# Parameter columns by a transposing DMA, stores of two chunks on ScalarE, and the skip product of chunk 0 on VectorE

## The chip, the cores and the metric

The kernel runs on one core of a Trainium2 chip. The metric is the device time of one execution in microseconds (us). Every ratio below compares a kernel with the kernel before on the same chip in the same rounds. The experiments ran in four such groups (e1 to e4, e5 to e8, e9 to e12, e13 and e14), each on another chip, so kernels of different groups are compared by their ratios. A run that takes over 1.5% more than the fastest of its own kernel is called slow and is left out of the ratio. A difference under 2% is called faster or slower only where the 95% interval of the ratio leaves out 1.

The words for the engines: TensorE is PE in the profile (PEld is its weight load), VectorE is DVE, ScalarE is ACT, GpSimd is POOL, SyncE is SP. A trailing q (ACTq, SPq, POOLq) is that engine's sequencer, which issues DMAs and waits for semaphores.

## The reference

```python
def reference(x, Lambda, B, C, log_dt, Dskip, w_gate, w_up, w_down):   # cut
    xn = layernorm(x)                        # 2048 tokens x 448
    dt = exp(log_dt); Lam_bar = exp(dt * Lambda)
    Bu = xn @ (((Lam_bar - 1) / Lambda)[:, None] * B).T
    h_t = Lam_bar * h_{t-1} + Bu_t           # complex scan over 2048 tokens
    s = 2 * real(h @ C.T) + xn * Dskip       # the last term is "the skip"
    g = silu((silu(xn @ w_gate) * (xn @ w_up)) @ w_down)   # F = 1792
    return x + s * g
```

## The kernel before

The 2048 tokens go through in four chunks of 512, each of four tiles of 128 tokens. Per chunk TensorE does the projections `pb` (input of the scan), the feed-forward pair `gp` and `up` ("gu"), the down product `hd` and the output sum `y`. Weights and states of 448 rows are split into 64-row halves of the array:

```python
def tell(mm):                       # a "notice": an empty instruction of GpSimd
    told = nc.gpsimd.nop(nofuse=True)
    tc.add_manual_dep(told.ins, mm.ins.name, SYNC, reason="share")
    return told.ins.name

def sums(q, pairs, between=None):   # cut: the two halves of the array take turns
    for share, first in ((0, True), (1, False)):
        for n, two in enumerate(pairs):
            for m in range(4 - share):
                for half in range(2):
                    mm = nc.tensor.matmul(...)
                    if not first and m == 0:
                        told_of(mm, left[n])      # second share waits for the notice
            if first:
                left.append(tell(mm))             # first share done: GpSimd passes it on
        if first:
            run_power()                           # one queued power, also on GpSimd
```

Every bank's second share waits until GpSimd has passed on a notice. GpSimd also computes the roots of the layer norm:

```python
def act_root(q):                    # sums come from ScalarE
    nc.gpsimd.tensor_scalar(out=vep[...], in0=sums_of[:, 1, :], ...)
    nc.gpsimd.tensor_tensor(out=rstd[...], in0=vep[...], in1=halves[:], op=ALU.pow)
    nc.gpsimd.tensor_tensor(out=off_of[:, 1, :], in0=off_of[:, 0, :], in1=rstd[...], op=ALU.mult)
```

The parameters (four rows of 448) are loaded as rows by GpSimd and turned into columns by six small transposes on TensorE, in the middle of `second_tokens`. The output tiles:

```python
def finish(q, j, y, sg, eng=nc.sync, c0=0, c1=D):       # cut
    t = work.tile(...)
    if (q, j) in SKIPS:                                  # chunks 1 to 3, not the last tile
        nc.vector.tensor_tensor(out=t[:], in0=y, in1=skip[q][:, j, c0:c1], op=ALU.add)
        y = t[:]
    nc.vector.tensor_tensor(out=t[:], in0=y, in1=sg[:, c0:c1], op=ALU.mult)
    ob = work.tile([P, c1 - c0], BF16, name="ob", **of)  # two buffers
    nc.vector.tensor_tensor(out=ob[:], in0=t[:], in1=x_all[:, m, c0:c1], op=ALU.add)
    eng.dma_start(out=out2d[m * P : (m + 1) * P, c0:c1], in_=ob[:])
```

For the tiles not in SKIPS, TensorE adds the skip itself with four matmuls against a diagonal, per tile. The middle of the schedule, in program order (cut):

```python
sg = downs(0, 1.8, {0: ..., 1: ..., 2: act_sums((10, 11), 1) + [on(act_root, 2), on(skips, 1)]})
bg.finish(0); turned_norms(8, 9, 10, 11)
outs(0, sg)                                             # stores by SyncE
sg = downs(1, 2.4, {0: act_sums((12, 13, 14), 0) + [on(skips, 2)],
                    1: act_sums((15,), 0) + [act_means] + act_sums((12, 13), 1),
                    2: act_sums((14, 15), 1) + [on(act_root, 3)]})
drive(2, 4.8)                                           # the projections pb of chunk 2
gu(2, bg, 2.4)
```

Of the kernel before, what the change touches and what calls it, by code (L numbers as in the profile page):

```python
# [10 lines left out]
ALU = mybir.AluOpType  # L11
ACT = mybir.ActivationFunctionType
BF16 = mybir.dt.bfloat16
F32 = mybir.dt.float32
# [30 lines left out]
def kernel(  # L45
# [43 lines left out]
    def blk(k):  # L89
        return slice(k * P, k * P + P) if k < KF else slice(D - P, D)  # L90
# [16 lines left out]
    def ctile(shape, dtype, name):  # L107
        return const.tile(shape, dtype, name=name)
# [13 lines left out]
    Id = ctile([P, P], BF16, "Id")  # L122
    CT = ctile([P, KT, W], BF16, "CT")
    ST = ctile([P, KT, W], BF16, "ST")
    vrow = ctile([4, D], BF16, "vrow")
    xn = [ctile([P, KT * P], BF16, f"xn{i}") for i in range(TQ)]
    pcol = ctile([P, KT + 1, 4], F32, "pcol")
    it_f = work.tile([P, W], F32, name="it_f", tag="row", bufs=1)
# [40 lines left out]
    natC = [work.tile([P, KT, D], BF16, name="natC", tag="nz") for _ in range(2)]  # L169
    nc.vector.memset(Wd[:, 0, :], 0.0)  # L170
    nc.vector.memset(Id[:], 0.0)
    nc.vector.memset(half_pi[:], math.pi / 2)
    for h, v in ((slice(0, R), TWO_PI), (slice(R, P), -TWO_PI)):
        nc.vector.memset(two_pi[h], v)

    def warm(n):
        t = bank("warm")
        for _ in range(n):
            nc.tensor.matmul(t[:, 0:D], lhsT=Wd[:, 0, 0:P], rhs=Wd[:, 0, :], start=True, stop=True)
# [76 lines left out]

    sums_of = ctile([P, 2, TQ], F32, "sums_of")
    off_of = ctile([P, 2, TQ], F32, "off_of")

    def act_sum(n, squares):  # L260
        i = n % TQ
# [33 lines left out]
    def ln_transpose(n):  # L295
        tp = bank("tp", BF16)
        for k in range(KT):
            nc.tensor.transpose(tp[:, block(k)], xn[n][:, blk(k)], Id[:])
        return tp

    def ln_evacuate(n, tp, eng):
        tp = tp[:, 0 : KT * P].rearrange("p (k c) -> p k c", k=KT)
        if eng is nc.scalar:
            nc.scalar.activation(xT_of(n), tp, ACT.Copy)  # L304
        else:
            nc.vector.tensor_copy(out=xT_of(n), in_=tp)
# [9 lines left out]
    dtv = vnew("dtv")  # L316
    b_re, b_im, nb_im = vnew("b_re"), vnew("b_im"), vnew("nb_im")

    def transpose_state(out, src, k, ident):

        if k < KF:
            nc.tensor.transpose(out, src[:, blk(k)], ident)
        else:
            for h in (slice(0, R), slice(R, P)):
                nc.tensor.transpose(out[h], src[:, KF * P : D], ident)

    def params_row(t):

        tv = t[:, KT * P : KT * P + 4 * (KT + 1)].rearrange("p (k r) -> p k r", r=4)
        for k in range(KT + 1):  # L330
            if k < KT:
                transpose_state(tv[:, k, :], vrow, k, Id[0:4, 0:4])
            else:
                nc.tensor.transpose(tv[:, k, :], vrow[:, blk(KF)], Id[0:4, 0:4])
        return tv

    def params_in():
        tt, ts = nc.vector.tensor_tensor, nc.vector.tensor_scalar
# [264 lines left out]
        return sg  # L603

    skip = {}
    SKIPS = [(q, j) for q in (1, 2, 3) for j in range(TQ)][:-1]

    def skips(q):

        skip[q] = work.tile([P, TQ, D], BF16, name="skip", tag="nz")  # L610
        for j in range(TQ):
            for c0, c1, x0 in ((0, KF * P, 0), (KF * P, D, KF * P + R)):
                nc.vector.tensor_tensor(
                    out=skip[q][:, j, c0:c1], in0=xn[j][:, x0 : x0 + c1 - c0],
                    in1=skip["row"][:, c0:c1], op=ALU.mult,
                )

    def out_sum(q, j, k0=0, k1=KT):

# [34 lines left out]
    def on(fn, *args):  # L654
        return lambda: fn(*args)
# [5 lines left out]
    for n in range(2):  # L661
        ln_norm(n)
        ln_evacuate(n, ln_transpose(n), nc.scalar)
        warm(1 + n)
    for n in range(2, TQ):
        ln_stats(n)
        ln_root(n, n + 1)
# [2 lines left out]

    def second_tokens():
        ln_evacuate(2, ln_transpose(2), nc.scalar)
        t = ln_transpose(3)
        tv = params_row(t)
        ln_evacuate(3, t, nc.vector)
        nc.scalar.activation(pcol[:], tv, ACT.Copy)
        power(dtv[:], euler[:], pcol[:, 0:KT, 0])

    CW = W // 2
# [37 lines left out]
    def drive(q, budget):  # L717
        bu_alloc(q)
        bu(q, (0, 1, 2), True, [on(table_sin, 3), params_trig] if q == 0 else ())
        if q == 0:  # L720
            params_out()
        ssm_steps(bg, q)
        bg.run(budget)

# [6 lines left out]
            bg.run(budget)  # L731
        return sg

    def outs(q, sg, hooks={}):
        for j in range(len(sg)):
            finish(q, j, out_sum(q, j), sg[j])
            for fn in hooks.get(j, ()):
                fn()

    def do(fns):  # L740
        for fn in fns:
            fn()

    gu(0, bg, 0.0, {
        0: [*stats(4, 5), on(params_in), on(table_phase, 0)],
# [15 lines left out]
    def act_sums(ns, squares):  # L761
        return [on(act_sum, n, squares) for n in ns]

    gu(1, bg, 2.2, {2: cw(0)[0], 3: cw(0)[1], 4: cw(1)[0], 5: cw(1)[1]})
    drive(1, 4.0)
    sg = downs(0, 1.8, {
        0: cw(2)[0] + cw(3)[0] + act_sums((8, 9), 0),
        1: act_sums((10, 11), 0) + [act_means] + act_sums((8, 9), 1) + cw(2)[1] + cw(3)[1],
        2: act_sums((10, 11), 1) + [on(act_root, 2), on(skips, 1)],
    })  # L770
    bg.finish(0)
    turned_norms(8, 9, 10, 11)
    outs(0, sg)
    sg = downs(1, 2.4, {
        0: act_sums((12, 13, 14), 0) + [on(skips, 2)],
        1: act_sums((15,), 0) + [act_means] + act_sums((12, 13), 1),
        2: act_sums((14, 15), 1) + [on(act_root, 3)],
    })
# [1 line left out]
    gu(2, bg, 2.4)  # L780
    bg.finish(1)
    turned_norms(12, 13, 14, 15)
    outs(1, sg)
    sg = downs(2, 2.4, {1: [on(skips, 3)]})
    drive(3, 4.8)
    gu(3, bg, 2.4)
    bg.finish(2)
# [36 lines left out]
```

## Time and profile before

| | before |
|---|---|
| median of 4 runs | 187.42 us (186.88 to 187.54) |
| span of the profiled run | 185.0 us, TensorE clock 1.000 |
| TensorE busy | 177.9 us, 96% |
| first pb / pb of chunk 2 / last y start at | 29.82 / 89.04 / 179.46 us |

The span is cut into 40 slices by the profile page, and each engine's busy share is given per slice; the timeline of one engine lists its instructions with start, duration and, in brackets, the idle time just before with the instruction that ended it. Two places of the kernel before are shown here because the result turns on them. The first is the table of stretches for the start (columns: stretch; busy time and count of PE, PEld, DVE, ACT, POOL; granted TensorE clock; DMA share; GB/s).

```profile
10.50:15.30 4.80, 4.71 (x68) 3.05 (x66) 2.88 (x7) 2.50 (x6) 1.02 (x1) 1.00 1.03 323
15.30:21.20 5.90, 5.88 (x58) 2.46 (x54) 5.62 (x18) 4.75 (x10) 1.19 (x1) 1.00 0.92 253
```

TensorE is busy in all of it at full clock, while the DMA engines are saturated with the weight loads. The second place is GpSimd's timeline around the third root.

```profile
88.92 1.01 POOL L278 TENSOR_TENSOR rstd<-vep,halves 128x4 f32<-128x4 f32 x1
90.00 0.22 POOL L281 TENSOR_TENSOR off_of<-off_of,rstd 128x4 f32<-128x4 f32 x1
```

```profile
89.04 5.47 PE L455 MATMUL pb<-xT,BT 64*128 64x512 bf16 x56
```

The projections of chunk 2 start at 89.04 us. Their first shares (16 of 56 matmuls) take at most 1.90 us, as the row of the changed kernel below shows, so TensorE needs the first notice shortly before 90.94. GpSimd dispatches the last instruction of the root at 90.00. The slack of that notice is therefore only some 0.8 us, an estimate from these starts.

### The profile page before, as it was taken

The page shows a single profiled execution, that of the slowest core. Times are in us where ns is not written, and L with a number is a line of the kernel's source. Part 1 is how long each engine was busy: PE and PEld are TensorE (multiplying, and loading weights), DVE is VectorE, ACT ScalarE, POOL GpSimd, SP SyncE. Part 2 cuts the span into 40 slices and gives each one's busy share as a digit, 9 for nine tenths or more (in the row PEclk, how much of TensorE's full clock was granted, in tenths as well). Part 3 has the DMA queues.
Part 4 walks back from the last instruction along what each step waited for, and adds up shares of the span by engine and source line. Part 5 has one row for each costly group of instructions (what it writes and reads, how often), then busy time and mean ns, then how long its engine had stood idle before and what let it go on. Part 6 is the DMA issues. An engine that isn't in the chain of part 4 may idle for free.

```text
span 185.0 us, 3723 instructions
## 1 busy us (share of the span) xinstructions
PE 177.9 (96%) x1449; PEld 87.8 (47%) x1449; DVE 160.1 (87%) x254; ACT 120.2 (65%) x247; POOL 13.4 (7%) x25
## 2 busy tenths in 40 slices
PE   7899999999999999999999999979999999999991
PEld 3574444544444555555454444535454444455551
DVE  4649799999999999902999999999999999999583
ACT  3247879997789999498499556962259696512110
POOL 7332200000000000600300000000000000000000
PEclk9999999999999999999999999999999999999999
DMA  5899655979200000043100000042100000001111
GB/s 160 209 277 338 124 94 112 132 167 377 101 0 0 5 0 0 0 86 81 50 2 4 2 0 4 0 82 70 62 4 0 0 4 0 0 4 50 50 50 50
DMA packets 26129, 12.71 MB, mean 69 GB/s; under 512 B 16000, under 2 KB 26112, under 8 KB 26112
## 3 DMA queue, kind: packets, MB, share of 16 engines
q1 hardware_dynamic: 24896, 12.06, 25.3%
q10 hardware_dynamic: 1088, 0.41, 0.8%
q8 instruction: 11, 0.18, 0.4%
q14 instruction: 6, 0.05, 0.1%
q0 software_dynamic: 128, 0.00, 0.0%
HBM read 7.23 MB, written 1.84 MB: 49 GB/s over the span
## 4 chain that ended last, share of the span: by engine, by line
PE 67%; DVE 25%; DMA 3%; issue 2%; ACT 1%; POOL 0%; SPq 0%; DVEq 0%
PE gp L455 20%; PE hd L597 16%; PE up L455 15%; PE pb L455 9%; PE y L626 7%; DVE bu_re L527 5%; DVE bu_im L527 4%; DVE tmp L521 2%; DVE Vt L589 2%; DVE ob L648 2%; DMA out_dram<-ob 2%; DVE t L645 2%; DVE H_im L521 2%; DVE ere L521 1%; DMA x_all<-in_A_x_dram 1%
## 5 line engine op out<-in xcount | busy, mean ns | idle before, releaser
L455 PE MATMUL gp<-xT,Wg 64*128 64x512 bf16 (+1 forms) x413 | 85.8, 365 | 0.4 <-ACT xT L304 0.3
L455 PE MATMUL up<-xT,Wu 64*128 64x512 bf16 (+1 forms) x413 | 85.8, 365 | 0.0
L455 PEld LDWEIGHTS <-Wg 64*128 64x128 bf16 x413 | 38.5, 94 | 25.1 <-issue 0.4
L455 PEld LDWEIGHTS <-Wu 64*128 64x128 bf16 x413 | 38.4, 94 | 19.7 <-POOLq L437 0.5
L581 ACT ACTIVATE gs<-gp 128x512 bf16<-128x512 f32 x56 | 33.7, 604 | 19.6 <-PE gp L455 11.7
L597 PE MATMUL hd<-Wd,Vt 128*128 128x448 bf16 x224 | 43.4, 353 | 1.3 <-DVE Vt L589 1.3
L585 ACT ACTIVATE us<-up 128x512 bf16<-128x512 f32 x54 | 32.9, 609 | 0.0
L597 PEld LDWEIGHTS <-Vt 128*128 128x128 bf16 x224 | 21.8, 98 | 22.0 <-DVE Vt L589 1.7
L602 ACT ACTIVATE sg<-hd 128x448 bf16<-128x448 f32 x16 | 8.6, 538 | 25.2 <-PE hd L597 20.6
L455 PE MATMUL pb<-xT,BT 64*128 64x512 bf16 (+1 forms) x224 | 21.9, 349 | 0.0
L648 DVE TENSOR_TENSOR ob<-t,x_all 128x448 bf16<-128x448 f32 (+2 forms) x17 | 10.2, 597 | 8.2 <-DMA out_dram<-ob 7.7
L589 DVE TENSOR_TENSOR Vt<-gs,us 128x2048 bf16<-128x2048 bf16 (+1 forms) x16 | 17.2, 1079 | 0.0
L455 PEld LDWEIGHTS <-BT 64*128 64x128 bf16 x224 | 10.7, 94 | 11.4 <-issue 0.7
L626 PE MATMUL y<-C,H_re 128*128 128x448 bf16 (+2 forms) x68 | 15.7, 342 | 0.0
L527 DVE TENSOR_TENSOR_SCAN bu_re<-rcol,H_re,ere 128x512 bf16<-128x512 f32 x12 | 14.9, 1262 | 0.1
L488 ACT ACTIVATE bu_re<-pb 128x512 bf16<-128x512 f32 (+1 forms) x20 | 10.1, 537 | 2.7 <-PE pb L455 2.6
L626 PE MATMUL y<-C,H_im 128*128 128x448 bf16 (+2 forms) x51 | 11.9, 342 | 0.0
L498 ACT ACTIVATE bu_im<-bu_re 64x512 bf16<-64x512 bf16 x16 | 10.0, 628 | 2.1 <-DVE bu_re L527 1.8
L527 DVE TENSOR_TENSOR_SCAN bu_im<-rcol,H_im,eim 128x512 bf16<-128x512 f32 x9 | 11.4, 1262 | 0.0
L287 ACT ACTIVATE xn<-x_all,off_of,rstd 128x384 bf16<-128x384 bf16 (+1 forms) x16 | 8.1, 588 | 2.8 <-POOL off_of L281 2.8
L521 DVE TENSOR_TENSOR tmp<-bu_im,ST 128x2048 bf16<-128x2048 bf16 x8 | 9.7, 1218 | 0.0
L626 PEld LDWEIGHTS <-H_re 128*128 128x128 bf16 x68 | 6.4, 98 | 6.1 <-issue 0.4
(98 smaller groups left out, 174.5 us busy)
## 6 DMA issues: line engine op xcount, KB each, us to landing
out_dram<-ob SPq DMA_DIRECT2D x15, 112.0 KB, 1.7
Wd<-in_B_w_down_dram SPq DMA_DIRECT2D x1, 1568.0 KB, 9.0
x_all<-in_A_x_dram SPq DMA_DIRECT2D x1, 896.0 KB, 5.5
Wg<-in_B_w_gate_dram SPq DMA_DIRECT2D x2, 384.0 KB, 7.0
Wu<-in_B_w_up_dram SPq DMA_DIRECT2D x2, 384.0 KB, 7.6
x_all<-in_A_x_dram SPq DMA_DIRECT2D x1, 448.0 KB, 5.7
Wg<-in_B_w_gate_dram SPq DMA_DIRECT2D x1, 288.0 KB, 3.1
Wu<-in_B_w_up_dram SPq DMA_DIRECT2D x1, 288.0 KB, 4.2
```

The source lines that it names most:

```text
L455: mm = nc.tensor.matmul(out, lhsT=w[h, d, :], rhs=xT[h, d, q * W + c0 : q * W + c1], start=(first and m == 0), stop=(not first and m == 3 ...
L488: nc.scalar.activation(to, pair[i][0], ACT.Copy)
L498: nc.scalar.activation(out[a], in_[b], ACT.Copy)
L521: nc.vector.tensor_tensor(out=of(out, n), in0=of(a, n), in1=of(b, n), op=op)
L527: nc.vector.tensor_tensor_scan(out=T["b"][c][:, k, :], data0=rcol[:, k : k + 1].to_broadcast([P, W]), data1=T["e"][c][:, k, :], initial=in ...
L581: nc.scalar.activation(gs[:, i + j, :], gp_[:], ACT.Silu)
L585: nc.scalar.activation(us[:, i + j, :], up_[:], ACT.Copy)
L589: nc.vector.tensor_tensor(out=Vt[:, f0 : f0 + n, :], in0=gs[:, 0:n, :], in1=us[:, 0:n, :], op=ALU.mult)
L597: nc.tensor.matmul(hd, lhsT=Vt_of[q][:, fi, j * P : (j + 1) * P], rhs=Wd[:, fi, :], start=(fi == 0), stop=(fi == NF - 1),)
L602: nc.scalar.activation(sg[:], hd, ACT.Silu)
L626: nc.tensor.matmul(y[:, c0:c1], lhsT=h, rhs=C2[:, n, c0:c1], start=(n == 0), stop=(n == NS - 1))
L648: nc.vector.tensor_tensor(out=ob[:], in0=t[:], in1=x_all[:, m, c0:c1], op=ALU.add)
```

## The change

The intent: take six small transposes and sixteen diagonal matmuls from TensorE, which is 96% busy, and take the stores of chunks 0 and 1 out of SyncE's queue, where they stand behind transposing DMAs and make VectorE wait 7.7 us for an output buffer.

```diff
-    vrow = ctile([4, D], BF16, "vrow")
+    vrow = work.tile([16, D], BF16, name="vrow", tag="ob")
+    vcol = ctile([P, KT, 16], BF16, "vcol")
...
+    nc.vector.memset(vrow[:], 0.0)
...
-    def transpose_state(...) / params_row(t): six nc.tensor.transpose      # cut
+    def turn_params():
+        for k, cols in ((slice(0, KF), slice(0, KF * P)), (slice(KF, KT), blk(KF))):
+            nc.scalar.dma_start(out=vcol[:, k, :], in_=vrow[:, cols], transpose=True)
+
+    def params_col():                      # four small ScalarE copies, cut
...
         ln_evacuate(n, ln_transpose(n), nc.scalar)
         warm(1 + n)
+    turn_params()
...
     def second_tokens():
         ln_evacuate(2, ln_transpose(2), nc.scalar)
-        t = ln_transpose(3)
-        tv = params_row(t)
-        ln_evacuate(3, t, nc.vector)
-        nc.scalar.activation(pcol[:], tv, ACT.Copy)
+        ln_evacuate(3, ln_transpose(3), nc.vector)
+        params_col()
         power(dtv[:], euler[:], pcol[:, 0:KT, 0])
...
-    SKIPS = [(q, j) for q in (1, 2, 3) for j in range(TQ)][:-1]
+    SKIPS = [(q, j) for q in range(NQ) for j in range(TQ)][:-1]
+    def first_norms():                     # four ScalarE normalisations of chunk 0, cut
...
-    sg = downs(0, 1.8, {
+    sg = downs(0, 1.3, {
...
-        2: act_sums((10, 11), 1) + [on(act_root, 2), on(skips, 1)],
+        2: act_sums((10, 11), 1) + [on(act_root, 2), on(skip_tile, 0), on(skip_tile, 1),
+                                    first_norms, on(skips, 1)],
+        3: [on(skips, 0)],
...
-    outs(0, sg)
+    outs(0, sg, nc.scalar)
...
-    outs(1, sg)
+    outs(1, sg, nc.scalar)
```

More of the change, by code (lines that the diff above doesn't have):

```diff
@@ L258 @@
     off_of = ctile([P, 2, TQ], F32, "off_of")
+    off_0 = ctile([P, TQ], F32, "off_0")
     def act_sum(n, squares):
@@ L317 @@
     b_re, b_im, nb_im = vnew("b_re"), vnew("b_im"), vnew("nb_im")
-    def transpose_state(out, src, k, ident):
-        if k < KF:
-            nc.tensor.transpose(out, src[:, blk(k)], ident)
-        else:
-            for h in (slice(0, R), slice(R, P)):
-                nc.tensor.transpose(out[h], src[:, KF * P : D], ident)
-    def params_row(t):
-        tv = t[:, KT * P : KT * P + 4 * (KT + 1)].rearrange("p (k r) -> p k r", r=4)
-        for k in range(KT + 1):
-            if k < KT:
-                transpose_state(tv[:, k, :], vrow, k, Id[0:4, 0:4])
-            else:
-                nc.tensor.transpose(tv[:, k, :], vrow[:, blk(KF)], Id[0:4, 0:4])
-        return tv
+    def turn_params():
+        for k, cols in ((slice(0, KF), slice(0, KF * P)), (slice(KF, KT), blk(KF))):
+            nc.scalar.dma_start(out=vcol[:, k, :], in_=vrow[:, cols], transpose=True)
+    def params_col():
+        last = vcol[:, KF, 0:4]
+        nc.scalar.activation(pcol[:, 0:KF, :], vcol[:, 0:KF, 0:4], ACT.Copy)
+        nc.scalar.activation(pcol[:, KT, :], last, ACT.Copy)
+        for h in (slice(0, R), slice(R, P)):
+            nc.scalar.activation(pcol[h, KF, :], last[R:P], ACT.Copy)
     def params_in():
@@ L605, with skip_tile @@
     skip = {}
-    SKIPS = [(q, j) for q in (1, 2, 3) for j in range(TQ)][:-1]
+    SKIPS = [(q, j) for q in range(NQ) for j in range(TQ)][:-1]
+    def skip_tile(q):
+        skip[q] = work.tile([P, TQ, D], BF16, name="skip", tag="nz")
     def skips(q):
-        skip[q] = work.tile([P, TQ, D], BF16, name="skip", tag="nz")
         for j in range(TQ):
-            for c0, c1, x0 in ((0, KF * P, 0), (KF * P, D, KF * P + R)):
+            parts = [(0, KF * P, 0), (KF * P, D, KF * P + R)] if q else [(0, D, 0)]
+            for c0, c1, x0 in parts:
+                normed = xn[j][:, x0 : x0 + c1 - c0] if q else skip[q][:, j, :]
                 nc.vector.tensor_tensor(
-                    out=skip[q][:, j, c0:c1], in0=xn[j][:, x0 : x0 + c1 - c0],
-                    in1=skip["row"][:, c0:c1], op=ALU.mult,
-                )
+                    out=skip[q][:, j, c0:c1], in0=normed, in1=skip["row"][:, c0:c1], op=ALU.mult
+                )
+    def first_norms():
+        for j in range(TQ):
+            nc.scalar.activation(
+                skip[0][:, j, :], x_all[:, j, :], ACT.Identity, bias=off_0[:, j : j + 1],
+                scale=rstd[:, j : j + 1],
+            )
     def out_sum(q, j, k0=0, k1=KT):
@@ L721, in drive @@
             params_out()
+            nc.vector.scalar_tensor_tensor(
+                out=off_0[:], in0=mv[:, 0:TQ, 0], scalar=-1.0, in1=rstd[:, 0:TQ],
+                op0=ALU.mult, op1=ALU.mult,
+            )
         ssm_steps(bg, q)
@@ L732, in downs, with outs @@
         return sg
-    def outs(q, sg, hooks={}):
+    def outs(q, sg, eng=nc.sync):
         for j in range(len(sg)):
-            finish(q, j, out_sum(q, j), sg[j])
-            for fn in hooks.get(j, ()):
-                fn()
-    def do(fns):
-        for fn in fns:
-            fn()
+            finish(q, j, out_sum(q, j), sg[j], eng)
     gu(0, bg, 0.0, {
@@ L772 @@
     turned_norms(8, 9, 10, 11)
-    outs(0, sg)
+    outs(0, sg, nc.scalar)
     sg = downs(1, 2.4, {
-        0: act_sums((12, 13, 14), 0) + [on(skips, 2)],
+        0: act_sums((12, 13, 14), 0) + [on(skip_tile, 2), on(skips, 2)],
         1: act_sums((15,), 0) + [act_means] + act_sums((12, 13), 1),
@@ L782 @@
     turned_norms(12, 13, 14, 15)
-    outs(1, sg)
-    sg = downs(2, 2.4, {1: [on(skips, 3)]})
+    outs(1, sg, nc.scalar)
+    sg = downs(2, 2.4, {1: [on(skip_tile, 3), on(skips, 3)]})
     drive(3, 4.8)
```

## The prediction

> **What bounds the kernel now.** I read the page's busy shares and slices first, then the list of waits, then the chain that ended last in order of time, then the timelines of single engines around the places which the chain named. The busy shares, and three rows of the waits:
>
> ```profile
> PE 177.9 (96%) x1449; PEld 87.8 (47%) x1449; DVE 160.1 (87%) x254; ACT 120.2 (65%) x247; POOL 13.4 (7%) x25
> ```
>
> ```profile
> DVE ob L648 <- DMA out_dram<-ob: 7.7, 1, 7.7
> ...
> PE hd L597 <- DVE Vt L589: 1.3, 1, 1.3
> ...
> PEld L455 <- POOLq L437: 0.5, 1, 0.5
> ```
>
> TensorE works 177.9 of 185.0 us, so a wait on another engine is worth only what reaches TensorE. Its idle time is 7.1 us; the stretches of the trace put 1.9 us of it before 16.4 us, 3.8 us after its last matmul (180.9 to 185.0), and 1.26 us in one wait in the middle, the second row. VectorE's 7.7 us wait is six times as long, but what TensorE loses by it can be no more than that 1.26 us. The chain in order of time ties the two together:
>
> ```profile
> 82.86 0.36 SPq L309
> 83.32 3.33 DMA out_dram<-ob
> 86.74 0.64 DVE ob L648
> ...
> 123.94 0.61 DVE Vt L589
> 124.60 8.50 PE hd L597 x44
> ```
>
> The third store buffer of chunk 0 waits for the first store, which stands in SyncE's queue behind four transposing DMAs, and these wait for ScalarE's normalisation. From 86.74 to 124.5 VectorE then works without a break, and TensorE waits for its last product Vt. Two timelines show the two ends (start, duration, instruction):
>
> ```profile
> 76.98 4.04 ACT L287 ACTIVATE xn<-x_all,off_of,rstd 128x384 bf16<-128x384 bf16 x8 [2.77 <-POOL off_of L281]
> 81.20 0.54 ACT L602 ACTIVATE sg<-hd 128x448 bf16<-128x448 f32 x1 [0.19 <-PE hd L597]
> ```
>
> ```profile
> 78.09 5.13 SPq L309 DMA_TRANSPOSE xT<-xn  x4
> 83.32 5.83 SPq L649 DMA_DIRECT2D out_dram<-ob  x4
> ```
>
> **What the Trainium skill says.** (1) "Perfetto Trace Analysis", section "DMA Instruction — HWDGE (DVE, Sync)": the issuing sequencer first waits for its semaphores and is free for its next instruction only when the descriptors are out. The trace agrees: the stores stand behind the transposes, each of which holds SyncE 1.2 us. So a store issued by ScalarE holds ScalarE until VectorE has the tile ready. (2) "DMA: Bandwidth & Descriptors", section "Issuing engines are not separate DMA queues": issuing elsewhere saves only issue time, as the data engines are shared. No bandwidth is won here; the stores land in 1.7 us (median) anyway. What is won is the place in the queue. (3) Same page, "Silent corruption: two transposing streams in flight at once": ScalarE's transposes must have landed before SyncE's first one. That one is issued at 17.7 us, so this should cost nothing. (4) "ScalarE: Activation LUTs", "What ACT_TABLE_LOAD costs": 280 ns + 0.833 ns a column with a bias by pointer, 93 ns for a further pointer. For 384 columns that is 693 ns; the trace has 697 for the normalisation. It agrees.
>
> **The change, part by part: the parameters.** Removed from TensorE: six tiny transposes, 9.74 to 10.12 us, 0.38 us. They sit on the path (the VectorE copy of the fourth tile waits 0.9 us for the last of them), so TensorE could run 0.38 us earlier. But the third row of waits cancels that: at 16.43 TensorE is released by a GpSimd notice, queued behind a power whose exponent VectorE finishes only at 16.31, after statistics of a tile that lands at 13.8. TensorE would come 0.38 us earlier and be released at the same 16.43. I count 0.
> Added: a zeroing of 16 x 448 on VectorE, an estimated 0.25 us from the like-sized first memset (245 ns), ahead of the parameter loads. GpSimd's loads move from 1.25 to about 1.5 us; its first root moves from 4.03 to 4.3 and ends by 4.9, when the second, which carries the path, starts. No cost. The last row then lands near 2.93 + 0.25 + 3.9 = 7.1 us, just as ScalarE ends its second tile (7.06). Two transposing issues at 1.25 us (SyncE's row: 1.2 to 1.3) hold ScalarE until 9.65, and its next tile started at 9.62: just fits. Transposes landed 2.4 us after issue in quiet times and 2.6 to 5.1 in loaded ones; with some 3.8, the second, issued at 8.4, lands at 12.2. Four small copies (187 ns each, overlapped, some 0.6 us) follow: the parameter columns are ready at 12.8 instead of 10.9, and the first Silu starts near 12.8 instead of 12.15. ScalarE catches up (65% busy in this loop). The power on GpSimd, dispatched at 12.01 before, blocks TensorE's second half-share only if it is dispatched after about 13.2. Even that is absorbed if TensorE still reaches the 16.43 release.
>
> **The skip of chunk 0.** Removed from TensorE: 16 diagonal matmuls. Their own durations (219 ns) overlap, so I take the spacing of whole tiles: 72.27, 73.79, 75.31, 76.83, that is 1.52 us with them; chunk 1, without them, runs at 1.32. Four times 0.20 is 0.80 us, on the bounding engine: gain 0.80.
> Added on ScalarE: four normalisations of 448 columns. From 697 ns at 384 columns and 480 at 128, 751 ns each, spaced 0.67 after overlap: 2.7 us, from 73.7 to 76.4, inside its 2.77 us idle before the 76.98 row. Added on VectorE: four products of an estimated 0.38 us (349 ns at 384 columns, 183 at 64) = 1.5 us, and four additions of 0.65 us = 2.6 us. The products follow ScalarE's normalisations, so VectorE, which by the smaller budget of 1.3 has less background to do before them, reaches them at 72.6 and ends them at 76.8: about 2.7 us of waiting. The tile in between (1.14) brings the finishes of chunk 0 to 78.0 instead of 75.6.
>
> **The stores.** Each finish now takes three steps, 2.04 us (as chunk 1 shows: 124.46, 126.50, 128.55). Output tiles are ready at 80.0, 82.0, 84.0 and 86.1. ScalarE ends its normalisations at 81.0, stores the first at once, and that lands near 82.8, before VectorE needs the buffer for its third tile (83.4). The 7.7 us wait goes. VectorE is left with: 7.7 removed, 1.5 + 2.6 + 2.7 added, and 0.4 us of former overlap with ScalarE lost, so it starts the scans only some 0.2 to 0.5 us earlier than 90.19. But two instructions of its background (2.1 us) now stand behind the last Vt instead of ahead of it; so that product comes about 2.3 us earlier, and the 1.26 us wait of TensorE goes: gain 1.26.
> The price lies on ScalarE: it waits for the fourth tile and is free at about 86.5, where it went on at 81.20 before. Its work up to the last Silu of chunk 1 is 7.1 us (8.48 from 81.20 to 89.68, less 1.2 of waits and some 0.1 between), so that ends at 93.6 instead of 89.7. TensorE, 0.8 us ahead, begins the next projections at 88.24; their last pair needs, after 3.02 + 0.86 us, the accumulator bank of that Silu: at 92.1. It waits 1.5 us. One thing softens it: the turn-over that made ScalarE wait for VectorE until 91.5 has moved behind the evacuations. For chunk 1 ScalarE is blocked until about 130.5, but TensorE needs those banks only at about 134.7: no cost.
>
> **Sum.** -0.80 - 1.26 + 1.5 = about -0.6 us, with nothing at the start.
>
> **The rivals.** (a) ScalarE becomes the bound: blocked by the stores for longer than I think, it delays every evacuation of chunk 2, and TensorE loses 3 us or more. For: 5 us of delay against a slack of 2.4 us in that Silu. Against: only one bank of eight is late, and ScalarE has a third of its time free later. Time 188 to 190. (b) ScalarE's delay is hidden, because the normalisations or the finishes come sooner: both gains stay, -2.1 us, 185.4; with the start as well, 185.0. For: GpSimd's slow power (1.99 us here, 1.01 the next time) may be short. (c) The transposed parameters land late, near 14 us: TensorE waits on the notice behind the power, 0.5 to 1 us, and 187 or more results. For: the DMA share is 0.93 from 9.2 to 13.9 us. Against: transfers on ScalarE's own queue landed in 3.4 to 4.0 us in such load. (d) Everything but the diagonal matmuls is hidden: -0.8 us.
>
> **Range and chances.** Taking (b) and (d) somewhat into account beside the sum, I expect -1.25 us: 187.45 - 1.25 = 186.2 us. All of TensorE's removable time is 0.80 + 1.26 + 0.38, about 2.5 us, so the low end is 184.6; one wrong wait of 2 us gives the high end, 187.9. Faster by over 2% needs 3.75 us, more than I find to remove: 0.04. Slower by over 2% needs rival (a) at full size: 0.04. Within 2%: 0.92.
>
> **What would show it.** No VectorE wait on a store in 79 to 87 us; chunk 0's output tiles on TensorE spaced 1.32 us; no wait of hd for Vt near 124; the Silu of chunk 1's first tile at about 86 instead of 81.2; a TensorE wait for a Silu in the projections near 92 us, of 1.5 us; the parameter copies near 12.8 and the release by GpSimd at about 16.4. The forecast fails if that TensorE wait is missing or several us long, if parameters arrive after 14 us, or if VectorE falls behind in the last chunk.

## The result, and the profile after

| | before | after |
|---|---|---|
| median of 4 runs | 187.42 us (186.88 to 187.54) | 198.88 us (197.9 to 200.26) |
| ratio after/before | | 1.062 (95%: 1.055 to 1.069) |
| span, clock of the profiled run | 185.0 us, 1.000 | 197.4 us, 0.965 |

A ratio is the mean time of one kernel's fast runs over the mean of the other's fast runs of the same rounds, so it is not quite the ratio of the medians. The change makes the kernel 6% slower, where 0.7% faster was expected.

The starts of TensorE's stages, from its timelines in both traces, show where the time came from:

| stage starts at | before | after | shift | new in this step |
|---|---|---|---|---|
| pb of chunk 0 | 29.82 | 37.13 | +7.31 | **+7.31** |
| y of chunk 0 | 72.27 | 79.58 | +7.31 | 0 |
| hd of chunk 1 | 78.35 | 84.88 | +6.53 | **-0.78** |
| pb of chunk 2 | 89.04 | 95.57 | +6.53 | 0 |
| gu of chunk 2 | 94.35 | 108.33 | +13.98 | **+7.45** |
| pb of chunk 3 | 133.03 | 145.57 | +12.54 | **-1.44** |
| last y | 179.46 | 192.00 | +12.54 | 0 |

The two gains came (0.78 and 1.44 us), and two losses of over 7 us each came with them. The page after, busy shares and TensorE's slices (in the clock row a 9 is 90% of full speed or more):

```profile
PE 181.1 (92%) x1427; PEld 91.5 (46%) x1427; DVE 164.8 (83%) x264; ACT 123.3 (62%) x254; POOL 13.1 (7%) x25
...
PE   7718999999999999999719999999999999999992
...
PEclk9995899999999999999967999999999999999999
```

TensorE has 22 fewer instructions and is busy for longer. Its row has two holes, in the third slice and in the twentieth and twenty-first, and after each the clock row falls (to 5 and to 6). The list of waits of TensorE in the changed kernel gives each hole a name (columns: who waited, for what; us in all, times, the longest):

```profile
PE pb L452 <- POOLq L434: 5.5, 1, 5.5
PE gp L452 <- ACT xT L307: 5.1, 2, 4.8
```

**The first hole.** ScalarE's third xT copy in the kernel before, then ScalarE's timeline at the start of the changed kernel, then TensorE's at the end of the hole:

```profile
9.62 0.60 ACT L304 ACTIVATE xT<-tp 128x512 bf16<-128x512 bf16 x1 [2.56 <-PE tp L298]
```

```profile
6.76 0.60 ACT L307 ACTIVATE xT<-tp 128x512 bf16<-128x512 bf16 x1 [0.26 <-PE tp L301]
11.52 3.09 ACTq L324 DMA_TRANSPOSE vcol<-vrow  x2
14.66 0.60 ACT L307 ACTIVATE xT<-tp 128x512 bf16<-128x512 bf16 x1 [7.31 <-issue]
18.18 0.21 ACT L329 ACTIVATE pcol<-vcol 128x12 f32<-128x12 bf16 x1 [2.92 <-DMA vcol<-vrow]
```

```profile
15.31 0.37 PE L452 MATMUL gp<-xT,Wg 64*128 64x256 bf16 x1 [4.77 <-ACT xT L307]
```

ScalarE was done with its second xT copy at 7.36, and the parameter rows had landed by about 7.4. Yet the first transpose was issued at 11.52, and the two were out only at 14.61. The third xT copy, for which TensorE waits, stood behind them until 14.66; the prediction had it at 9.65. What the transposes waited for is in the built program, in the list of semaphores ahead of each instruction. The completions of all DMAs of SyncE and ScalarE are counted by eight counters in rotation, and a DMA that takes over a counter first waits until the counter's previous user has landed. The first transpose takes a counter last used by a 288 KB load of Wu, issued at 7.29, which landed near 11.4; the second takes that of the 448 KB load of x, issued at 8.24, which landed at 13.47. Neither has anything to do with the parameters. The chain that ended last in the changed kernel, in order of time, goes through the second of them:

```profile
8.24 5.23 DMA x_all<-in_A_x_dram
...
13.50 1.12 ACTq L324
...
14.66 0.61 ACT xT L307
```

The stretches of the changed kernel, to set beside those of before:

```profile
10.50:15.30 4.80, 0.04 (x2) 0.09 (x1) 0.06 (x1) 0.60 (x1) 0.00 (x0) 0.91 1.07 359
15.30:21.20 5.90, 5.89 (x48) 4.18 (x49) 3.18 (x10) 1.91 (x6) 1.02 (x1) 0.50 0.76 203
```

The compute engines all but stand for nearly 5 us (ScalarE works 0.60 us of it), and then TensorE works for some 6 us at half its clock. This is what the Trainium skill, "TensorE: Matmul & The Clock Gate", section "HAM oscillation — how this bites in real kernels", warns of: an idle gap beyond about 3.4 us throttles the clock to half. This trace agrees: 4.77 us idle, then 0.50. So a wait of 4.8 us cost 7.3. (A shorter wait is not always safe: see e8 below.)

**The second hole.** ScalarE, then GpSimd, then TensorE, in the changed kernel:

```profile
89.19 4.50 ACTq L657 DMA_DIRECT2D out_dram<-ob  x3
93.75 0.54 ACT L599 ACTIVATE sg<-hd 128x448 bf16<-128x448 f32 x1 [5.68 <-DVE ob L656]
...
100.26 0.53 ACT L599 ACTIVATE sg<-hd 128x448 bf16<-128x448 f32 x1
```

```profile
100.44 0.42 POOL L277 TENSOR_SCALAR vep<-sums_of 128x4 f32<-128x4 f32 x1 [17.57 <-ACT junk L266]
100.95 1.90 POOL L281 TENSOR_TENSOR rstd<-vep,halves 128x4 f32<-128x4 f32 x1
102.93 0.29 POOL L284 TENSOR_TENSOR off_of<-off_of,rstd 128x4 f32<-128x4 f32 x1
```

```profile
95.57 1.90 PE L452 MATMUL pb<-xT,BT 64*128 64x512 bf16 x16
102.97 1.46 PE L452 MATMUL pb<-xT,BT 64*128 64x512 bf16 x6 [5.50 <-POOLq L434]
```

ScalarE holds three stores from 89.19 to 93.69, as VectorE makes the tiles 2 us apart. Its sums for chunk 3 therefore end near 100.3, and the root on GpSimd runs from 100.44. TensorE needs nothing of that root before the next chunk. But it needs the notice that stands behind the root in GpSimd's queue, and gets it at 102.97 where it wanted it near 97.4. The clock falls again. The projections take 12.76 us instead of 5.31: 5.50 of wait, and about 1.9 because what was left took 5.36 us (102.97 to 108.33) instead of some 3.4 (5.31 less 1.90), at a clock of 0.66 in the mean.

### The profile page after: what moved, and what is told of

Its sections match the earlier page's. It is cut to its first block, busy times and chain, and to the rows that moved or that the text cites. A ratio compares the mean times of both kernels' runs of the same rounds, so it can differ in the third digit from the quotient of the medians.

```text
span 197.4 us, 3696 instructions
## 1 busy us (share of the span) xinstructions
PE 181.1 (92%) x1427; PEld 91.5 (46%) x1427; DVE 164.8 (83%) x264; ACT 123.3 (62%) x254; POOL 13.1 (7%) x25
## 4 chain that ended last, share of the span: by engine, by line
PE 71%; ACT 9%; DVE 8%; DMA 5%; issue 2%; SPq 2%; POOL 1%; ACTq 1%; DVEq 0%; POOLq 0%
PE gp L452 25%; PE up L452 19%; PE pb L452 11%; PE hd L594 11%; PE y L634 6%; ACT junk L266 5%; DMA x_all<-in_A_x_dram 3%; DVE ob L656 3%; DVE t L653 3%; DVE t L651 2%; DMA Wg<-in_B_w_gate_dram 2%; ACT skip L621 1%; ACT c_tb L416 1%; ACT sg L599 1%; POOL rstd L281 1%
## 5 line engine op out<-in xcount | busy, mean ns | idle before, releaser
L452 PE MATMUL gp<-xT,Wg 64*128 64x512 bf16 (+1 forms) x413 | 88.6, 375 | 5.1 <-ACT xT L307 5.1
L452 PE MATMUL up<-xT,Wu 64*128 64x512 bf16 (+1 forms) x413 | 88.5, 375 | 0.0
L452 PEld LDWEIGHTS <-Wg 64*128 64x128 bf16 x413 | 40.0, 97 | 24.7 <-issue 0.9
L452 PEld LDWEIGHTS <-Wu 64*128 64x128 bf16 x413 | 39.8, 97 | 23.7 <-issue 5.4
L578 ACT ACTIVATE gs<-gp 128x512 bf16<-128x512 f32 x56 | 33.6, 603 | 15.3 <-PE gp L452 15.2
L452 PE MATMUL pb<-xT,BT 64*128 64x512 bf16 (+1 forms) x224 | 23.8, 368 | 5.5 <-POOLq L434 5.5
L452 PEld LDWEIGHTS <-BT 64*128 64x128 bf16 x224 | 11.7, 98 | 17.9 <-POOLq L434 6.0
L634 PE MATMUL y<-C,H_re 128*128 128x448 bf16 (+2 forms) x68 | 15.1, 342 | 0.0
L651 DVE TENSOR_TENSOR t<-y,skip 128x448 f32<-128x448 f32 x15 | 9.4, 624 | 3.2 <-PE y L634 2.0
L524 DVE TENSOR_TENSOR_SCAN bu_im<-rcol,H_im,eim 128x512 bf16<-128x512 f32 x9 | 11.4, 1264 | 0.0
L653 DVE TENSOR_TENSOR t<-t,sg 128x448 f32<-128x448 f32 x15 | 9.4, 625 | 0.8
```

What stands on the lines that cost most here:

```text
L452: mm = nc.tensor.matmul(out, lhsT=w[h, d, :], rhs=xT[h, d, q * W + c0 : q * W + c1], start=(first and m == 0), stop=(not first and m == 3 ...
L524: nc.vector.tensor_tensor_scan(out=T["b"][c][:, k, :], data0=rcol[:, k : k + 1].to_broadcast([P, W]), data1=T["e"][c][:, k, :], initial=in ...
L578: nc.scalar.activation(gs[:, i + j, :], gp_[:], ACT.Silu)
L634: nc.tensor.matmul(y[:, c0:c1], lhsT=h, rhs=C2[:, n, c0:c1], start=(n == 0), stop=(n == NS - 1))
```

## The experiments

Fourteen kernels ran. All gave correct results. For each: its edit, what was expected, what was measured.

### Which part costs what: e1 to e4

e1 is the changed kernel with the parameters back on TensorE:

```diff
-    turn_params()
...
+        t = ln_transpose(3); tv = params_row(t)          # as before
+        nc.scalar.activation(pcol[:], tv, ACT.Copy)
```

> The changed kernel with the parameter rows transposed by TensorE again (four rows, six tiny transposes), everything else changed. My theory after seeing the changed trace: two separate stalls of TensorE, one near 10.5 us from the transposing DMAs on ScalarE (7.31 us together with the halved clock behind it) and one near 97 us from ScalarE's stores (7.45 us). So this run keeps only the second: 198.9 - 7.3 = 191.6 us, no TensorE wait over 1 us before 30 us, and a wait for a GpSimd notice of about 5 us near 90 us. Rival: the second stall is a consequence of the first (everything shifted); then it goes too and the time is about 185.

Measured: 193.77 us (192.16 to 194.18) against 187.15 of before, ratio 1.033 (1.027 to 1.039). That is 2 us more than expected. In the profiled run 0.8 us of this lies in the projections of chunk 2, which lost 8.26 us (88.59 to 102.16, against 5.31) and not 7.45; 0.3 us came before them (first pb at 30.16), and 0.8 us after the last y, where the last store took 2.2 us to land instead of 1.5. TensorE's longest wait is the notice:

```profile
PE pb L456 <- POOLq L438: 5.5, 1, 5.5
```

e2 is the changed kernel with the stores back on SyncE:

```diff
-    outs(0, sg, nc.scalar)
+    outs(0, sg)
-    outs(1, sg, nc.scalar)
+    outs(1, sg)
```

> The changed kernel with the stores of chunks 0 and 1 issued by SyncE again; the parameters by DMA and the skip of chunk 0 on VectorE stay. My theory: the 5.5 us wait for the GpSimd notice in the projections of chunk 2 comes from the stores holding ScalarE, so it goes, and the start keeps its 4.8 us wait. VectorE waits again for a store buffer, so TensorE waits for Vt later, about 3 us: 198.9 - 7.45 + 1.4 + 3 = about 195.8 us. Rival: the four normalisations and the longer finishes of chunk 0 are to blame for ScalarE's lateness; then the notice wait stays at 3 us or more and the time is 198 or more.

Measured: 192.46 us, ratio 1.028 (1.023 to 1.032). That is 3 us below what was expected. The miss is in the wait for Vt: I had added 4.4 us for it (1.4 and 3), and it came back at its old 1.3 us; 198.9 - 7.45 + 1.4 would have been 192.9. The notice wait is gone, the first hole is there, and the old wait for Vt is back:

```profile
PE gp L452 <- ACT xT L307: 5.1, 2, 4.7
PE hd L594 <- DVE Vt L586: 1.3, 1, 1.3
```

e3 has both edits: what is left of the change is the skip of chunk 0 on VectorE.

> Only the skip of chunk 0 on VectorE (with the smaller background budget); parameters by TensorE, stores by SyncE as before. My theory: TensorE saves 0.78 us in the outputs of chunk 0, but VectorE still waits for a store buffer (until about 86.7 us) and has 4 us more to do, so TensorE waits about 3 us for the last Vt of chunk 2 instead of 1.26: 187.4 - 0.8 + 1.8 = about 188.5 us. Rival: the background moved behind that Vt by the budget hides it, and the gain of 0.8 stays: 186.6.

Measured: 186.26 us (186.25 to 186.44), ratio 0.995 (0.991 to 0.999). Its rival's figure (186.6) was the nearer one. The output stage of chunk 0 takes 5.30 us instead of 6.08, and nothing else moved on TensorE: the wait for Vt is still 1.3 us.

e4 is the kernel before with the parameter change alone.

```diff
+    turn_params()                                       # vrow, vcol, params_col as in the change
```

> The kernel before with the parameter rows made columns by the transposing DMAs, nothing else. My theory: the whole loss of the start, +7.3 us: 194.7 us, with a TensorE wait of about 4.8 us for the third tile and a halved clock for some 6 us after it. Rival: half of that loss comes from the other parts (a later store of the zeroed rows' buffer, the added normalisations); then it is under +5 us.

Measured: 193.48 us, ratio 1.032 (1.028 to 1.037), 1.2 us below what was expected; TensorE waits 5.9 us for the third xT copy and runs at 0.50 of the clock from 15.3 to 21.2. The old wait for Vt, 1.3 us, is not in its list of waits, which is about what the expectation missed.

In per cent of before, the skip is -0.5, the parameters on top of it +3.3 (e2 less e3), the stores on top of it +3.8 (e1 less e3). The sum is +6.6; the whole change measured +6.2. So, within the intervals, the two losses add up, and each can be studied alone.

### What holds ScalarE at the start: e5, e9, e10, e13

The theory: the transposes wait for counters that they share with unrelated loads. e5 wrote the last thirteen loads after the transposes in the source, to free the counters:

```diff
-    load_gu(C1, 768)
-    load_x(TQ, 2 * TQ)
-    landed = load_gu(768, 1280)
-    load_gu(1280, F)
-    load_b(landed)
...
     turn_params()
+    (the same five lines)
```

> The changed kernel, except that the last 13 loads (weights from column 384 on, the second x tile group) are written after the parameter transposes instead of ahead of them. SyncE's own order stays; what changes is which of the eight rotating completion counters the two transposing DMAs take over. My theory: in the changed kernel they wait for the landings of the loads that used these counters before (a 288 KB weight load and the 448 KB x load, 11.5 and 13.5 us); here they take counters of loads that landed by 6 us, so the first is issued when the rows have landed, at about 7.5 us, ScalarE is free near 10 us, TensorE waits under 0.6 us at its third tile and keeps its full clock: 198.9 - 6.8 = about 192 us. Rival: the transposes are held by the descriptor generator or the full data engines; then they are still issued after 10 us and the time stays over 196.

Measured: 199.25 us, ratio 1.063, no change. The listing of the built program says why: the counters are dealt out in the order in which the build schedules the DMAs, and not in source order, so the transposes waited for the same two loads as before. This was a null edit, and it says nothing about the theory.

e9 and e10 go the other way. They leave the kernel before as it is and add two or three plain loads of eight bytes, whose result nobody reads, at the place of the transposes. In the built program the second one takes the counter last used by a 96 KB piece of Wu, the third that of the 448 KB load of x.

```diff
         warm(1 + n)
+    for i in range(2):                                  # e10: range(3)
+        nc.scalar.dma_start(out=tiny[0:1, 4 * i : 4 * i + 4], in_=A_log_dt[0:4].unsqueeze(0))
```

> The kernel before with two plain 8-byte loads (four values of a parameter row, read by nobody) issued by ScalarE where the changed kernel issues its two transposes. In the built program they wait for the completion counters whose last users are the 96 KB piece of Wg (lands near 10.0 us) and the 96 KB piece of Wu (issued 7.56, landed near 12.1). Theory, that a load holds ScalarE through the counter that it shares with an unrelated load: ScalarE is held to about 12.1, its third xT copy moves from 9.6 to about 12.5, TensorE stands for some 2.9 us[...]; 188.6 to 190.0 us. Rival, that it is the transposing or the landing of the parameter rows: two plain loads cost their issue alone, 187.3 to 188.0 us.

> The same with a third such load, whose counter was last used by the 448 KB load of x (landed near 13.7). Theory: ScalarE is held to about 13.8, the third xT copy starts near 14.2, TensorE stands for some 4.6 us and then runs at half clock for a few us, as in the changed kernel; 191 to 193 us. Rival: 187.3 to 188.2 us.

Measured: e9 190.15 us (188.24 to 190.69), ratio 1.016 (1.011 to 1.020); e10 191.75 us (191.05 to 192.86), ratio 1.027 (1.023 to 1.030), both against 186.87. e10 is in the range of the theory and far from the rival's. e9's median is just above its range, but its four runs lie apart: the profiled one, 188.24, is nearer to the rival's range (up to 188.0) than the other three. ScalarE's timelines, e9 and then e10:

```profile
9.24 2.56 ACTq L667 DMA_DIRECT2D tiny<-in_A_log_dt_dram  x2
11.84 0.60 ACT L305 ACTIVATE xT<-tp 128x512 bf16<-128x512 bf16 x1 [4.51 <-DMA Wu<-in_B_w_up_dram]
```

```profile
9.44 3.98 ACTq L667 DMA_DIRECT2D tiny<-in_A_log_dt_dram  x3
13.47 0.60 ACT L305 ACTIVATE xT<-tp 128x512 bf16<-128x512 bf16 x1 [6.39 <-DMA x_all<-in_A_x_dram]
```

The bracket says it: ScalarE's next copy was released by the landing of Wu in e9 and of x in e10, and one load more, of eight bytes, moved the copy by 1.63 us. No transpose and no parameter row is involved, so the rival (that transposing itself, or the rows, are at fault) is not needed for this wait. Nor was issuing itself blocked: in the changed kernel SyncE issued six loads between 8.72 and 12.16 us, while ScalarE stood. e10 also shows when the clock falls: its wait on TensorE was 3.48 us and ended at 14.12, the clock is 1.00 up to 15.3 and 0.70 from 15.3 to 21.0, that is, after the work had resumed. In e9 the wait was 1.6 us in the profiled run (I had expected 2.9), which left the clock at 1.000 and took 188.24 us; its other three runs had 0.988 to 0.989 and took 189.8 to 190.7; they have no trace, so where their clock fell is not shown.

e13 asks what is left of e4's loss if ScalarE is not the issuer. SyncE issues the two transposes after the load of x and ahead of the eight weight loads that followed it, and everything that needs the columns is one pair of feed-forward tiles later (cut):

```diff
-            nc.scalar.dma_start(out=vcol[:, k, :], in_=vrow[:, cols], transpose=True)
+            nc.sync.dma_start(out=vcol[:, k, :], in_=vrow[:, cols], transpose=True)
...
-    landed = load_gu(768, 1280)                          # written ahead of the transposes
-    load_gu(1280, F)
-    load_b(landed)
...
     turn_params()
+    (the same three lines)
...
-        params_col(); power(dtv[:], ...)                 # in second_tokens
-        0: [*stats(4, 5), on(params_in), on(table_phase, 0)],
+        0: stats(4, 5),
+        1: [params_turned, on(params_in), on(table_phase, 0)],
```

> The kernel before with the parameter change alone (as e4, 193.5 us), but the two transposes issued by SyncE after the 448 KB load of x, and the ScalarE copies that need their result, with the power and the phases that need those, one pair of feed-forward tiles later. Theory, that e4's loss is ScalarE held behind loads: the third xT copy is back near 9.8 us, TensorE has no wait of some us there and keeps its clock; the transposed columns land at 16 to 17.5 us, the copies and the power behind them hold ScalarE and the notices for up to 1.5 us; 187 to 189 us. Rival, that the transposes cost their time through the DMA engines or through their late landing, whoever issues them: 191 us or more.

Measured: 186.98 us (186.72 to 187.16), ratio 0.998 (0.996 to 1.000), just below the range expected. The whole loss of e4 (ratio 1.032) is gone. SyncE's issue and ScalarE's two copies:

```profile
9.19 2.45 SPq L320 DMA_TRANSPOSE vcol<-vrow  x2
```

```profile
9.69 0.60 ACT L303 ACTIVATE xT<-tp 128x512 bf16<-128x512 bf16 x1 [2.56 <-PE tp L297]
...
15.70 0.23 ACT L325 ACTIVATE pcol<-vcol 128x12 f32<-128x12 bf16 x1
```

The third xT copy is back at 9.69, and the columns are there before ScalarE asks for them: its copies follow at 15.70 without a wait. TensorE keeps two waits for a notice, of 1.0 us together, behind the power that needs the columns. The edit changes three things at once: the issuer, the order of the eight loads (the DMA share from 10.5 to 15.3 us is 0.75, in e4 1.05), and, by the list of the built program, the counters: the transposes take over those of two pieces of Wu issued at 2.79 and 4.16 us. So e13 shows that neither the transposing nor the rows are at fault by themselves, and not which of the three removed the loss.

### What the clock costs: e11

e11 is e4 with 48 throw-away matmuls in the hole, so that TensorE waits no less but is not idle:

```diff
     def first_pair():
+        for _ in range(48):
+            nc.tensor.matmul(first[0][0][:, CW:W], lhsT=Wd[:, 0, 0:P], rhs=Wd[:, 0, 0 : W - CW],
+                             start=True, stop=True)
```

> The kernel before with the parameter change alone (e4, 193.5 us), and 48 throw-away matmuls of 256 columns (0.108 us each, 5.2 us) ahead of the matmuls that wait for the xT copy, so that TensorE is busy while ScalarE is held. Theory, that the loss is idle time plus a clock that the idle time halves: the wait stays (it is filled), the clock stays at 1.00, and the some 2.1 to 3 us that gu(0) took longer go: 190.5 to 191.5 us. Rival, that the low clock has another cause, such as the DMA load: 193.5 us.

Measured: 191.71 us (191.35 to 192.17), ratio 1.026 (1.024 to 1.028), just above the range expected. A stretch of it, and its longest wait on TensorE:

```profile
15.30:21.20 5.90, 4.01 (x57) 2.84 (x56) 3.03 (x8) 2.10 (x7) 0.80 (x1) 1.00 0.62 185
```

```profile
PE up L451 <- POOLq L433: 1.7, 1, 1.7
```

The clock stays at 1.00 where e4 has 0.50, though the DMA share is nearly the same (1.04 against 1.05 from 10.5 to 15.3 us, 0.62 against 0.69 here), so the low clock comes from the idle time. From the end of the hole to the first pb, e4 needs 21.70 us (16.05 to 37.75) and e11 20.85 (15.70 to 36.55), of which 1.75 are a new wait: the notice now stands behind the power on GpSimd that needs the late columns, until 20.45. Without it e11 would need 19.1, so the low clock is worth 2.6 us. (The kernel before, from its matmul at 10.71 to the first pb at 29.82, needs 19.1 as well.) That, with the 4.77 us of wait, makes up the 7.3 of the first hole. The total fell by 0.6% only, some 1.2 us, as a later wait took the place of the gain.

### What holds TensorE in the middle: e6, e7

e6 is e1 with one edit: the third root is issued a few tiles later, in the feed-forward of chunk 2, behind the notices of the projections.

```diff
-        2: act_sums((14, 15), 1) + [on(act_root, 3)],
+        2: act_sums((14, 15), 1),
...
-    gu(2, bg, 2.4)
+    gu(2, bg, 2.4, {3: [on(act_root, 3)]})
```

> Parameters by TensorE, stores by ScalarE, skip of chunk 0 on VectorE (as e1), but GpSimd's root of chunk 3 is queued in the middle of chunk 2's gate loop instead of ahead of the notices of chunk 2's projections. My theory: in e1 TensorE waits 5.5 us because its notice stands in GpSimd's queue behind that root, which waits for sums that ScalarE makes late; here that wait goes and the wait which my prediction named (an accumulator bank, 1.5 us near 92 us) is what is left, if anything: 193.8 - 7.4 + 0 to 1.5 = 186.4 to 187.9 us. Rival: ScalarE's lateness itself is the stall; then TensorE still waits 3 us or more near 90 us and the time is over 189.

Measured: 187.20 us (186.62 to 187.82), ratio 1.000 (0.997 to 1.003), where e1 has 1.033. TensorE in the projections of chunk 2:

```profile
93.33 1.57 PE L456 MATMUL pb<-xT,BT 64*128 64x256 bf16 x19 [1.09 <-ACT sg L603]
```

The 5.5 us wait is gone, and under it appears the wait that the prediction had: the last pair of projections waits for the bank of chunk 1's last Silu, 1.09 us. The stage takes 6.57 us, 1.26 more than before.

e7 is the changed kernel with the edits of e5 and e6 together; as the first is void, it is the changed kernel with the late root.

> The changed kernel with both mends (loads written after the parameter transposes, root of chunk 3 later); all three parts of the change are in. My theory: no stall of TensorE over 1.5 us is left, full clock throughout; the gains forecast are there (0.8 us of diagonal matmuls, 1.3 us of the wait for Vt): 185.5 to 187.5 us. Rival: an interaction which neither mend covers leaves it over 189.

Measured: 193.39 us, ratio 1.031 (1.027 to 1.035), against 1.062 of the change as it was. Its waits:

```profile
PE gp L447 <- ACT xT L302: 6.3, 2, 6.0
...
PE pb L447 <- ACT sg L594: 1.1, 1, 1.1
```

It is not the 185.5 to 187.5 us that two mended parts would have given, as only one was mended. The first hole is untouched, the second is gone. The two losses are separate here too.

### What is left of the idea: e8, e12, e14

e8 starts from e3 and frees VectorE from the stores in another way: the output tile is written over the skip product, which is no longer needed, so no buffer is shared with a store in flight, and SyncE may be late.

```diff
-        ob = work.tile([P, c1 - c0], BF16, name="ob", **of)
+        if (q, j) in SKIPS:
+            ob = skip[q][:, j, c0:c1]
+        else:
+            ob = work.tile([P, c1 - c0], BF16, name="ob", **of)[:]
```

> Skip of chunk 0 on VectorE, parameters by TensorE, stores by SyncE (as e3), and the output tile is written over the tile's own skip product, so that no store buffer is waited for. My theory: VectorE's remaining 1.8 us wait on a store goes, and with it TensorE's 1.3 us wait for Vt in chunk 2, with no load on ScalarE: 186.3 - 1.3 = 185.0 us. Rival: VectorE meets TensorE's output tiles earlier and waits for those instead, or Vt stays late: then it stays at 186.

Measured: 188.93 us (187.04 to 189.62) in the five fast runs of six, ratio 1.007 (1.003 to 1.011): slower. The sixth, 190.15, was a slow run. The chain of waits:

```profile
86.10 2.80 DMA out_dram<-skip
...
89.08 1.57 DVE skip L618 x8
```

The skip product of chunk 2 takes the room of chunk 0's (there are two), so it waited for chunk 0's last store to land. The wait had only moved, and TensorE's wait for Vt grew to 2.0 us. (The list of waits puts these 3.0 us down to a Silu; the instruction waits for four DMA counters and ScalarE alike, and both came within 0.1 us of each other.)

TensorE's longer wait is the smaller part of the loss. The two stretches after it (columns as above):

```profile
125.20:126.40 1.20, 1.20 (x7) 0.65 (x8) 1.13 (x3) 0.00 (x0) 0.00 (x0) 0.99 0.51 104
126.40:129.60 3.20, 3.20 (x10) 1.24 (x9) 2.92 (x5) 1.80 (x3) 0.00 (x0) 0.50 0.12 38
```

The wait of 2.02 us ends at 125.19, and 1.2 us later the clock is at 0.50 for 3.2 us. The matmuls of hd after the wait take 10.11 us instead of 8.42 in e3, so the clock cost 1.7 us and the longer wait 0.75. The runs fit: the one with a mean clock of 1.000 took 187.04 us, the other five had 0.989 to 0.991, and 0.991 is what 3.2 us at half clock make of a span of 187.3 (an estimate, 1 - 1.6/187.3).

e12 adds to e8 that this product is issued three tiles later:

```diff
-        0: act_sums((12, 13, 14), 0) + [on(skip_tile, 2), on(skips, 2)],
+        0: act_sums((12, 13, 14), 0),
...
+        3: [on(skip_tile, 2), on(skips, 2)],
```

> Skip alone (e3, 186.3 us, its measured ratio 0.995), with the output written over the skip product as in e8, so that no buffer is shared with a store, and the skip product of chunk 2 three tiles later, so that it does not wait for chunk 0's stores as in e8. Theory: neither of VectorE's waits is left, the wait of hd for Vt (1.3 us) goes, 185.0 us. Rival: the skip product of chunk 2 now stands ahead of chunk 1's scan and moves the wait to TensorE: 186 us or more.

Measured: 185.27 us (185.03 to 185.67), ratio 0.992 (0.990 to 0.993): faster, as is e14. The waits for Vt and for stores are gone. One wait is new: 0.5 us for a notice in the projections of chunk 2.

e14 adds the late root of e6.

> e12 (185.3 us), in which TensorE still waited 0.5 us for a notice behind the third root on GpSimd, with that root moved into the third feed-forward block as in e6. Theory: the wait of 0.5 us goes and no other takes its place: 184.7 us. Rival: the bank wait for ScalarE behind it, hidden so far, takes over: 185.3 us.

Measured: 184.49 us (184.36 to 185.07), ratio 0.985 (0.983 to 0.987). The projections of chunk 2 then run without a break:

```profile
88.13 5.47 PE L456 MATMUL pb<-xT,BT 64*128 64x512 bf16 x56
```

This is the best version that ran: 1.5% faster than the kernel before. It keeps the skip on VectorE and leaves stores on SyncE and parameters on TensorE.

## Why the prediction was wrong

- **"I count 0" for the parameters: this step failed, by 7.3 us.** The prediction let ScalarE issue the transposes as soon as the rows had landed, near 7.1, and gave them 2 x 1.25 us: "just fits". The rows did land near 7.4. But the issues waited for the landing of two unrelated loads, until 14.61, and the next copy came at 14.66, not at 9.65. It quoted the rule that an issuer first waits for its semaphores, and asked only for those of the data; e9 and e10 show the others.
- **The idle time's second price was missing.** No term of the sum had a clock in it. The hole of 4.77 us cost some 2.6 us more at half clock (worked out in e11), and the hole in the middle some 1.9.
- **"They hold ScalarE ... the last Silu ends at 93.6": right within 0.7 us.** With the shift of 6.53 us by that point this makes 100.1; that Silu ran from 100.26 to 100.79.
- **"It waits 1.5 us": this step failed in the changed kernel.** The prediction asked which bank is late, and not who else waits for ScalarE's delayed sums. GpSimd's root does, and the notice behind it had some 0.8 us of slack. The cost was 7.45 us instead of 1.5. The bank wait that it forecast is real, 1.09 us with the stage 1.26 us longer, and shows once the root is moved (e6).
- **The gains were right.** Diagonal matmuls: 0.80 forecast, 0.78 measured (the output tiles are 1.32 us apart). Wait for Vt: 1.26 forecast; the wait is gone, and the step that held it is 1.44 us shorter. VectorE's wait for a store near 83 us is gone. With the holes' causes out of the way (e6) the last y starts 1.05 us earlier than before, where the sum was 0.6; its time is that of before nonetheless, as its tail after that point was 0.75 us longer in the profiled run (6.29 against 5.54 us): its last store took 2.3 us to land instead of 1.5.
- **Of the rivals,** the third (columns land late, TensorE waits on the notice behind the power) exists: 1.75 us in e11, 1.0 us in e13, hidden behind the first hole in the changed kernel. The first, ScalarE as the bound, was near the truth in its sign, but ScalarE was 62% busy: it was held, not full.
- **The range's ends do not follow from the sums beside them:** 187.45 - 2.5 is 184.95 and not 184.6, and one wrong wait of 2 us on 186.2 is 188.2 and not 187.9. Two losses of over 7 us each lay outside either.

What stays open: the counter was not taken away from the transposes on ScalarE (e5 was void), so the case for it rests on the list of the built program, on adding the wait (e9, e10) and on e13, which changed issuer, counters and the order of loads together. How short a wait is safe for the clock is open too (e8, e9). e13 and e14 were not combined.

## What to carry to other kernels

Before moving a DMA's issue to a busy compute engine, list all that the issue waits for, the completion counters that it shares with loads in flight included, and then all that stands behind it in that engine's queue. When an engine will be late, follow each of its results to its consumers, and ask what stands behind those consumers in their own queues: a relay such as a notice on GpSimd has only the slack of what precedes it. And put a price on TensorE's idle time that includes the clock: here every hole of 4.8 to 5.5 us cost 2 to 2.6 us more, and in e8 a wait of 2.0 us was followed by a low clock that cost 1.7 us.

## What the Trainium skill lacked or had wrong

- "DMA: Bandwidth & Descriptors", section "Why a DMA increments its semaphore by 16 and not by 1", asks for one semaphore per in-flight slot. It doesn't say what that costs when there are more DMAs in flight than semaphores: an issue then waits for the landing of another engine's load. Here two 8-byte loads took ScalarE 2.56 us to issue, and three 3.98 us (e9, e10).
- "TensorE: Matmul & The Clock Gate", section "HAM oscillation — how this bites in real kernels", asks for no idle gap over about 3.4 us. The long gaps agree (4.77 us idle gave 0.50 here), but a shorter one was not safe: in e8 a wait of 2.02 us was followed by 3.2 us at 0.50, and five of its six runs had a mean clock of 0.989 to 0.991. The runs add that the clock can fall after the work has resumed (e10: 1.00 up to 15.3 us, then 0.70, with the wait over at 14.12; e8: 1.2 us after the wait).
- No page speaks of GpSimd as a relay between TensorE's two shares, and of what a late instruction ahead of the relay costs: 5.50 us of wait here, behind a root whose sums came 3 us after TensorE wanted the notice and whose three instructions took 2.6 us.
- No page gives a measured time that the transpose of so small a tile as 16 rows, from SBUF to SBUF, holds the sequencer: 2.45 us for two of them, and 4.0 us (median) to landing, in e13.
